# Experts' arms issued in source order: half blocks first, w2's low parts on VectorE, named PSUM banks, one tile moved behind the branch

## The chip, the cores and the metric

One core of one Trainium2 chip runs the whole program. The metric is device microseconds of an execution; lower is better. Times of before are 825.06 to 826.63 us, median 825.95 us of three runs.

## The reference

Causal attention with a bias (8 batches, 8 heads, 576 positions, 64 per head) gives 4608 tokens of 512 numbers. Each token then goes through one of eight experts, the one with the largest gate logit:

```python
for e in range(E):                       # E = 8, D = 512, F = 1024
    mask = e_idx == e
    h = np.maximum(x[mask] @ w1[e], 0.0)
    ye = h @ w2[e]
    out[mask] = gate_w[mask, None] * eom[mask, e, None] * ye
```

All of it is float32.

## The kernel before

The attention and the routing come first, in an order written by a planner (`Order`); they end at about 380 us and the change doesn't touch them. The experts then run one after the other.

**Number format.** To multiply in float32 on TensorE (PE) each operand is split into a high part and a low part of a shorter format, and three products are added: high by high, high by low, low by high. ScalarE (ACT) makes the high part with a cast, another engine the low part with a subtraction. `xh`, `xl` are the tokens (transposed), `hh`, `hl` the hidden values, `w1h`, `w1l` and `w2h`, `w2l` the weights (some tiles of both weights carry the bare name `w` in the profile). `w1r` and `w2r` are the weights as loaded, with one buffer each.

**One expert** has a front (`front`, line 1173) and a back (`back`, 1222). How many tokens an expert has is known only on the chip, so the front stands in a `Switch` with nine arms, for 512 to 768 tokens in steps of 32 (`ARMS`). Tile t is tokens 128t to 128t + 127.

- `gemm1` (847), first product: for each of NF = 8 row blocks f, 4 x 3 = 12 matmuls per half. More than 512 columns are cut into two halves u, each in its own PSUM bank of the tile `ph` (two buffers of two banks).
- `relu` (860) empties `ph`: part "h" on ACT writes `hh`, part "l" on VectorE (DVE) writes `hl`.
- `split_w2(f)` (1116) makes this expert's w2 parts from `w2r`: the cast on ACT, the subtraction on GpSimd (POOL). `split_w1(f)` (807) makes the next expert's w1 parts: the cast on ACT, the subtraction on DVE. It overwrites the parts that row block f of this expert has just used.
- `gather` (820, POOL) fetches tile f of the next expert's tokens by an indirect DMA.
- `gemm2` (1130), second product of a tile: 24 matmuls of 512 columns into a PSUM bank `py` (two buffers, taken in turn), then DVE scales it into `y` (1141), then POOL scatters `y` by an indirect DMA (1121). `gemm2_few` (1152) does a last tile of 32 or 64 tokens with the roles turned round; POOL first adds `hh` and `hl` into `hf` (1160).
- `load_w2(e + 1)` and `load_w1(e + 2)` are issued by SyncE (SP) once their buffers' readers are done.

**Front and back.** If there are more than 640 tokens (T > LT = 5) the front first transposes tile 5 (`ready`: PE transposes into `pt`, ACT makes `xh`, DVE `xl`). Then come the eight row blocks and the second product of tile 0 and of the tiles from 4 on (for expert 0, whose tiles 0 to 2 are prepared within the attention's plan, of tile 3 and those from 4 on). The back, behind the branch, does the second product of tiles 1, 2 and 3 (expert 0: tile 2), and between the matmuls of the last two it transposes the next expert's tiles 0 to 4.

**The order of the work.** The back is issued in source order (`manual_schedule`, 1239). The front is not: within an arm the framework's scheduler chooses each engine's order by its own cost model. Every engine runs its own queue in that order. Each engine takes the branches for itself, into an arm and out of it.

In this execution the experts have 544, 512, 512, 672, 704, 512, 576 and 640 tokens of room; experts 0, 3, 4 and 6 have a narrow tile.

Of the kernel before, what the change touches and what calls it, by code (L numbers as in the profile page):

```python
# [10 lines left out]
F32 = mybir.dt.float32  # L11
# [7 lines left out]
P = 128  # L19
# [192 lines left out]
def moe_attention(ctx, tc, q, k, v, s, wg, wog, w1, w2, out):  # L212
# [577 lines left out]
    def w2_lo(f, eng):  # L790
        eng.tensor_sub(w2f("l", f), w2r[:, f], w2f("h", f).bitcast(F32))  # L791
# [15 lines left out]
    def split_w1(f):  # L807
        w1_hi(f)
        w1_lo(f, nc.vector)
# [34 lines left out]
        xcopy_h(t, p)  # L844
        xcopy_l(t, p)

    def gemm1(f, c0, c1, p):

        nh = 1 if c1 - c0 <= 512 else 2
        W = (c1 - c0) // nh  # L850
        for u in range(nh):
            us = slice(c0 + u * W, c0 + (u + 1) * W)
            n = 0
            for c in range(ND):
                for a, b_ in (("h", "xh"), ("h", "xl"), ("l", "xh")):
                    nc.tensor.matmul(p[:, u, 0:W], w1f(a, f)[:, c, :], wt[b_][:, c, us],  # L856
                                     start=(n == 0), stop=(n == 3 * ND - 1))
                    n += 1

    def relu(f, c0, c1, p, part):  # L860
        nh = 1 if c1 - c0 <= 512 else 2
        W = (c1 - c0) // nh
        pv = p[:, 0:nh, 0:W]
        hv, lv = (wt[nm][:, f, c0:c1].rearrange("p (u w) -> p u w", u=nh) for nm in ("hh", "hl"))
        if part == "h":
            nc.scalar.activation(hv, pv, AF.Relu)  # L866
        else:
            nc.vector.scalar_tensor_tensor(lv, pv, 0.0, hv.bitcast(F32), ALU.max, ALU.subtract)  # L868
# [68 lines left out]
    def hint(e):  # L937
        tc.switch_hint({g: regs[e] for g in ENGINES}, (1 if e else 2) * NA, f"expert{e}")
# [176 lines left out]

    def split_w2(f):
        w2_hi(f)
        w2_lo(f, nc.gpsimd)

    def place(dst, ix, y):  # L1120
        ins = nc.gpsimd.indirect_dma_start(  # L1121
# [5 lines left out]
    def scatter(y, tb, t, m):  # L1127
        place(out, tb.bitcast(I32)[0:m, t, 1:2], y[0:m])

    def gemm2(e, t, C, between=((),)):  # L1130

        m = min(P, C - t * P)
        p = pm.tile([P, DM], F32, tag="py", name="py")
        n = NF // len(between)
        for k, steps in enumerate(between):
            for step in steps:
                step()
            product2(t, m, p, range(k * n, (k + 1) * n))
        y = mw.tile([P, DM], F32, tag="y", name="y", bufs=3)
        tb = tbs[e % 2]  # L1140
        nc.vector.tensor_scalar_mul(y[0:m], p[0:m], tb[0:m, t, 2:3])  # L1141
        scatter(y, tb, t, m)
# [6 lines left out]
        nc.sync.dma_start(tb, tab[r0:r0 + m, :].unsqueeze(0).broadcast_to([G, m, 3]))  # L1149
        return tb  # L1150

    def gemm2_few(t, m, tb):

        G = P // m
        W = DM // G
        ix = mw.tile([P, 1], I32, tag="ixf", name="ixf", bufs=2)
        nc.vector.tensor_scalar(ix, tb.bitcast(I32)[:, 1:2], float(G), grp[m], ALU.mult, ALU.add)
        hf = wt["hf"][:, :, 0:m]
        sl = slice(t * P, t * P + m)
        nc.gpsimd.tensor_add(hf, wt["hh"][:, :, sl].bitcast(F32), wt["hl"][:, :, sl].bitcast(F32))  # L1160
        p = pm.tile([P, DM], F32, tag="py", name="py")
        for f in range(NF):
            for g in range(G):
                nc.tensor.matmul(p[g * m:(g + 1) * m, 0:W], hf[:, f], w2r[:, f, g * W:(g + 1) * W],  # L1164
                                 start=(f == 0), stop=(f == NF - 1))
        y = mw.tile([P, DM], F32, tag="y", name="y", bufs=3)
        nc.vector.tensor_scalar_mul(y[:, 0:W], p[:, 0:W], tb[:, 2:3])
        place(out.rearrange("n (g w) -> (n g) w", g=G), ix, y[:, 0:W])

    def ready(t, xg):  # L1170
        xcopy(t, xtrans(xg, pm.tile([P, ND, P], F32, tag="pt", name="pt")))

    def front(e, C, early=False):


        nxt = e + 1 < E
        T = (C + P - 1) // P
        few = C % P if C % P in grp else 0
        if e == 0 and not early:
            for t in range(ET):  # L1180
                ready(t, gather(tbs[0], t, xgs[t]))
        if T > LT:
            ready(LT, wt["last"])
        c0 = min(ET * P, C - 256) if early else 0
        if few:
            places = few_places(e, T - 1, few)
        if nxt and e > 0:
            load_tab(e + 1)
        if early:
            for t in range(EY):  # L1190
                scatter(banks["ye", t], tbs[0], t, P)
        for f in range(NF):
            p = pm.tile([P, 2, 512], F32, tag="ph", name="ph")
            gemm1(f, c0, C, p)
            for part in "hl":
                relu(f, c0, C, p, part)
            if e > 0:
                split_w2(f)
            if nxt:
                split_w1(f)  # L1200
                if f < TMAX:
                    gather(tbs[(e + 1) % 2], f, xgs[f])
        if not few and nxt:
            run_all(load_w2(e + 1))
        if nxt and e + 2 < E:
            run_all(load_w1(e + 2))

        tiles = ([0] if e else [ET] if early else [ET] + list(range(EY))) + list(range(NC, T))
        if few:
            tiles.remove(T - 1)  # L1210
            tiles.insert(1, T - 1)
        for k, t in enumerate(tiles):
            if few and t == T - 1:
                gemm2_few(t, few, places)
                if nxt:
                    run_all(load_w2(e + 1))
            else:
                gemm2(e, t, C)

    xgs = {}  # L1220

    def back(e):

        if e == 0:
            where = {EY: ((0, 1), (2,), (3,), (4, "hint"))}
        else:
            where = {1: ((),), 2: ((0,), (1,)), 3: ((2,), (3,), (4,), ("hint",))}
        for t, parts in where.items():
            gemm2(e, t, CMAX, [[(lambda u=u: hint(e + 1) if u == "hint" else ready(u, xgs[u])) for u in part
                                if e + 1 < E] for part in parts])  # L1230

    rest = nc.values_load(rgi[0:1, 2 * E:2 * E + 1], min_val=0, max_val=E * NOV,
# [1 line left out]
    for e in range(E):  # L1234
        if e + 1 < E:
            xgs.update((t, xg_tile(t)) for t in range(TMAX))
        for n in tc.Switch(regs[e], (1 if e else 2) * NA, hint=f"expert{e}"):
            front(e, ARMS[n % NA], early=e == 0 and n < NA)
        with tc.manual_schedule():
            if e + 1 < E:  # L1240
                regs[e + 1] = arm_of(e + 1)
            back(e)


    with tc.If(rest > 0):
        for e in range(E):
            rv = nc.values_load(rgi[0:1, E + e:E + e + 1], min_val=0, max_val=NOV,
                                skip_runtime_bounds_check_because="counted by comparisons")
            run_all(load_w1(e))
            run_all(load_w2(e))  # L1250
            with tc.For_i(0, rv, 1) as it:
                tb = mw.tile([P, 1, 3], F32, tag="tbo", name="tbo")
                nc.sync.dma_start(tb, tab[bass.ds(it * P + (e * N + CMAX), P), :].unsqueeze(1))
                xg = sh.tile([P, DM], F32, tag=XGS[0], name="xg", bufs=1)
                nc.gpsimd.indirect_dma_start(
                    out=xg, out_offset=None, in_=xd,
                    in_offset=bass.IndirectOffsetOnAxis(ap=tb.bitcast(I32)[:, 0, 0:1], axis=0),
                    bounds_check=N, oob_is_err=False)
                p = pm.tile([P, ND, P], F32, tag="pt", name="pt")
                for c in range(ND):  # L1260
                    nc.tensor.transpose(p[:, c, :], xg[:, c * P:(c + 1) * P], ident)
                xt = sh.tile([P, ND, P], F32, tag=XGS[1], name="xto", bufs=1)
                nc.vector.tensor_copy(xt, p)
                ho = sh.tile([P, NF, P], F32, tag="kq", name="ho")
                for f in range(NF):
                    p = pm.tile([P, 2, 512], F32, tag="ph", name="ph")
                    for c in range(ND):
                        nc.tensor.matmul(p[:, 0, 0:P], w1r[:, c, f * P:(f + 1) * P], xt[:, c, :],
                                         start=(c == 0), stop=(c == ND - 1))
                    nc.vector.tensor_scalar_max(ho[:, f, :], p[:, 0, 0:P], 0.0)  # L1270
                p = pm.tile([P, DM], F32, tag="py", name="py")
                for f in range(NF):
                    nc.tensor.matmul(p, ho[:, f, :], w2r[:, f], start=(f == 0), stop=(f == NF - 1))
                y = mw.tile([P, DM], F32, tag="y", name="y", bufs=3)
                nc.vector.tensor_scalar_mul(y, p, tb[:, 0, 2:3])
                scatter(y, tb, 0, P)
# [26 lines left out]
```

## Time and profile before

| | us |
|---|---|
| median of 3 runs | 825.95 |
| profiled execution | 824.76 |
| its span, first to last instruction | 823.0 |
| PE busy | 772.9 |
| DVE busy | 473.3 |
| POOL busy | 467.1 |
| ACT busy | 441.9 |
| mean granted clock of PE, share of 2.4 GHz | 0.978 |

A record's line in order of time gives its start, its length, engine, line, operation, what it writes and reads, and, in brackets, how long the engine stood idle just before it and what ended that. Matmuls are pipelined: records overlap, so a loss of PE is read from start to start. "issue" is idle time for which the profile shows no cause; it shows above all behind the branches. Times are from the start of the span.

### The profile page before, as it was taken

To read this page: it belongs to the slowest core of one execution; us is meant where nothing else is said; L and a number is where in the kernel's file an instruction comes from. 1 tells how busy PE (TensorE), PEld (TensorE's weight loads), DVE (VectorE), ACT (ScalarE), POOL (GpSimd) and SP (SyncE) were. 2 spreads that over 40 slices of the span, in tenths; PEclk is the share of its full clock that TensorE was granted. 3 is DMA by queue.
4 is the path that set the end of the run, shared out by engine and by line. 5 is a ranking of instruction groups with operands and counts; after the bars stand their busy time and mean duration, and the time that the engine had idled before them with its cause. 6 is when DMAs were issued, how large, how long until landed. Compare 5 with 4: busy or idle time off the path is not lost.

```text
span 823.0 us, 19429 instructions
## 1 busy us (share of the span) xinstructions
PE 772.9 (94%) x6854; PEld 610.8 (74%) x6854; DVE 473.3 (58%) x1310; ACT 441.9 (54%) x1277; POOL 467.1 (57%) x691
## 2 busy tenths in 40 slices
PE   4799999999999999898979999999899999989996
PEld 2577767676777676597867877897797887978985
DVE  4688888889988889772436353251352263442211
ACT  2699999999999999741333241430431341512300
POOL 7688798988888788464226172542262171631401
PEclk9699999999999999998999999999999999999998
DMA  4878688988897884333534427216126137214001
GB/s 124 197 194 202 159 217 209 231 171 201 189 224 181 187 176 117 82 118 93 175 131 133 179 79 247 58 48 237 54 66 215 61 78 252 68 40 142 14 29 42
DMA packets 168898, 115.61 MB, mean 140 GB/s; under 512 B 128090, under 2 KB 146524, under 8 KB 168670
## 3 DMA queue, kind: packets, MB, share of 16 engines
q1 hardware_dynamic: 160590, 91.06, 42.3%
q0 software_dynamic: 8080, 22.08, 8.7%
q8 instruction: 73, 1.20, 0.6%
q14 instruction: 155, 1.27, 0.5%
HBM read 93.59 MB, written 19.65 MB: 138 GB/s over the span
## 4 chain that ended last, share of the span: by engine, by line
PE 72%; issue 12%; DVE 5%; POOL 4%; DMA 3%; ACT 1%; SPq 1%; another core or an unknown queue 1%; POOLq 0%; DVEq 0%; ACTq 0%
PE ph L856 17%; PE py L892 16%; PE O L574 9%; PE S L482 9%; PE PT L543 6%; PE S L485 4%; PE M L597 4%; PE A L404 2%; PE pt L833 2%; PE O L570 1%; POOL w L791 1%; POOL out_dram L1121 1%; PE py L1164 1%; DMA raw<-in_q_dram 1%; POOL w2l L791 1%
## 5 line engine op out<-in xcount | busy, mean ns | idle before, releaser
L1121 POOL DMA_INDIRECT out_dram<-y,tb x34 | 33.6, 989 | 195.0 <-DVE y L1141 165.9
L892 PE MATMUL py<-w,hh 128*128 128x512 f32 x420 | 133.7, 399 | 5.7 <-DVE y L1141 5.1
L482 PE MATMUL S<-kq 64*128 64x256 f32 (+3 forms) x512 | 107.7, 473 | 3.0 <-DVE m L496 2.1
L856 PE MATMUL ph<-xh,w1h 128*128 128x512 f32 (+6 forms) x312 | 105.5, 338 | 5.1 <-DVE hl L868 4.3
L856 PE MATMUL ph<-xl,w1h 128*128 128x512 f32 (+6 forms) x312 | 104.4, 335 | 3.5 <-DVE xl L841 3.4
L856 PE MATMUL ph<-xh,w1l 128*128 128x512 f32 (+6 forms) x312 | 104.2, 334 | 0.0
L837 ACT CAST xh<-pt 128x512 fp32r<-128x512 f32 x37 | 21.6, 587 | 150.7 <-PE pt L833 145.3
L892 PEld LDWEIGHTS py<-w,hh 128*128 128x128 f32 x420 | 76.6, 189 | 23.4 <-DVE y L1141 7.6
L414 ACT COPY pt<-PT 128x256 f32<-128x256 f32 (+4 forms) x261 | 90.4, 415 | 4.0 <-PE PT L543 2.5
L1141 DVE TENSOR_SCALAR y<-py,tb 128x512 f32<-128x512 f32 x33 | 24.8, 751 | 106.7 <-PE py L892 100.8
L543 PEld LDWEIGHTS PT<-ident,e 64*128 64x128 f32 x1600 | 72.2, 143 | 17.8 <-issue 8.4
L805 DVE TENSOR_TENSOR w1l<-w1r,w1h 128x512 fp32r<-128x512 f32 x46 | 54.0, 1177 | 50.4 <-ACT w1h L802 50.3
L574 PE MATMUL O<-pt,vraw 128*64 128x448 f32 (+2 forms) x512 | 82.9, 467 | 0.0
L892 PE MATMUL py<-w,hl 128*128 128x512 f32 x210 | 82.7, 394 | 0.0
L543 PE MATMUL PT<-ident,e 64*128 64x64 f32 x1600 | 77.9, 228 | 1.6 <-DVE m L496 0.9
L791 POOL TENSOR_TENSOR w<-w2r,w 128x512 fp32r<-128x512 f32 x47 | 61.1, 1312 | 19.1 <-ACT w L788 8.9
L868 DVE SCALAR_TENSOR_TENSOR hl<-ph,hh 128x512 fp32r<-128x512 f32 (+6 forms) x72 | 50.3, 701 | 35.1 <-ACT hh L866 30.2
L518 ACT ACTIVATE e<-pbB,m 128x384 f32<-128x384 f32 (+1 forms) x128 | 67.4, 529 | 3.5 <-DVE m L496 3.5
L856 PEld LDWEIGHTS ph<-xh,w1h 128*128 128x128 f32 x312 | 60.3, 193 | 11.2 <-issue 6.1
L856 PEld LDWEIGHTS ph<-xl,w1h 128*128 128x128 f32 x312 | 60.4, 193 | 7.0 <-DVE xl L841 4.3
L574 PEld LDWEIGHTS O<-pt,vraw 128*64 128x64 f32 x512 | 36.2, 139 | 38.9 <-issue 31.0
L802 ACT CAST w1h<-w1r 128x512 fp32r<-128x512 f32 x48 | 29.4, 619 | 65.6 <-issue 56.0
(180 smaller groups left out, 1831.3 us busy)
## 6 DMA issues: line engine op xcount, KB each, us to landing
cb<-cumd SPq DMA_DIRECT2D x31, 576.0 KB, 5.8
w1r<-in_moe_w_dram SPq DMA_DIRECT2D x7, 2048.0 KB
w2r<-in_moe_w_dram SPq DMA_DIRECT2D x7, 2048.0 KB, 9.8
raw<-in_k_dram SPq DMA_DIRECT2D x64, 128.0 KB, 4.3
raw<-in_q_dram SPq DMA_DIRECT2D x64, 128.0 KB, 4.1
vraw<-in_v_dram SPq DMA_DIRECT2D x64, 128.0 KB, 6.2
xd<-x SPq DMA_DIRECT2D x32, 256.0 KB, 4.9
w1r<-in_moe_w_dram SPq DMA_DIRECT2D x4, 512.0 KB, 7.2
```

Of the source, the lines that this page charges most:

```text
L414: nc.scalar.copy(out, in_)
L482: nc.tensor.matmul(d["s", t, j][:, 0:width(t)], qt[js, t * P:(t + 1) * P], kt[js, TL:TL + width(t)], start=True, stop=True)
L485: nc.tensor.matmul(d["s", t, a][js, 0:HS], d["ql"][js], kt[js, a * HS:(a + 1) * HS], start=True, stop=True)
L518: nc.scalar.activation(e[:, o:o + W], pbias(i, t, j), AF.Exp, bias=st[i].pop(("m", t, j)), scale=-1.0, accum_out=sums[i % 3][:, j, t:t + 1])
L543: nc.tensor.transpose(p[h][:, (n0 + n) * D:(n0 + n + 1) * D], d[etile(t, j)][hs, o:o + P], ident[hs, hs])
L574: nc.tensor.matmul(d["o", 1][j * D:(j + 1) * D, q0 - P:S - P], vt[:, j, c, :] if c < NM else vls[i // NPAIR % 2][:, i % NPAIR, j], pt[:, c ...
L791: eng.tensor_sub(w2f("l", f), w2r[:, f], w2f("h", f).bitcast(F32))
L805: eng.tensor_sub(w1f("l", f), w1r[:, :, f * P:(f + 1) * P], w1f("h", f).bitcast(F32))
L856: nc.tensor.matmul(p[:, u, 0:W], w1f(a, f)[:, c, :], wt[b_][:, c, us], start=(n == 0), stop=(n == 3 * ND - 1))
L868: nc.vector.scalar_tensor_tensor(lv, pv, 0.0, hv.bitcast(F32), ALU.max, ALU.subtract)
L892: nc.tensor.matmul(p[0:m], wt[a][:, f, sl], w2f(b_, f), start=(f == 0 and n == 0), stop=(f == NF - 1 and n == 2))
L1121: ins = nc.gpsimd.indirect_dma_start(out=dst, out_offset=bass.IndirectOffsetOnAxis(ap=ix, axis=0), in_=y, in_offset=None, bounds_check=dst ...
```

## The change

Within the experts only.

1. The arms are put under `manual_schedule`: issued in source order, like the back.
2. The order in an arm is written anew: `split_w2(f)` ahead of `gemm1(f)`, relu directly behind it, then `split_w1(f)` and the gather. With more than 640 tokens and two halves, the first halves of row blocks 0 and 1 go first, then their second halves; `gemm1` and `relu` take a list of halves for that.
3. The low part of w2 is made by DVE, not by POOL.
4. `py` becomes two tiles of one buffer each, `py0` and `py1`, chosen by number so that an arm's last tile has bank 0 and the first tile behind the branch bank 1.
5. Tile 3 of expert 0 moves from the arm (for the usual arms) to the back, ahead of tile 2.
6. POOL's sum for the narrow tile is cut into two, behind row blocks 5 and 7.

```diff
-        for u in range(nh):
+        for u in range(nh) if halves is None else halves:
...
     def split_w2(f):
         w2_hi(f)
-        w2_lo(f, nc.gpsimd)
+        w2_lo(f, nc.vector)
+
+    def ybank(n):
+        return pm.tile([P, DM], F32, tag=f"py{n % 2}", name="py", bufs=1)
...
+    def few_rows(t, m, f0, f1):
+        sl = slice(t * P, t * P + m)
+        nc.gpsimd.tensor_add(wt["hf"][:, f0:f1, 0:m], wt["hh"][:, f0:f1, sl].bitcast(F32), wt["hl"][:, f0:f1, sl].bitcast(F32))
...
-        nc.gpsimd.tensor_add(hf, wt["hh"][:, :, sl].bitcast(F32), wt["hl"][:, :, sl].bitcast(F32))
-        p = pm.tile([P, DM], F32, tag="py", name="py")
+        p = ybank(bank)
...
-        for f in range(NF):
+
+        def split(f):
+            if nxt:
+                split_w1(f)
+                if f < TMAX:
+                    gather(tbs[(e + 1) % 2], f, xgs[f])
+            if few and f in (5, NF - 1):
+                few_rows(T - 1, few, *((0, 6) if f == 5 else (6, NF)))
+
+        first = []
+        if T > LT and C - c0 > 512:
+
+            first = [0, 1]
+            p = [pm.tile([P, 2, 512], F32, tag="ph", name="ph") for f in first]
+            for u in range(2):
+                for f in first:
+                    if u and e > 0:
+                        split_w2(f)
+                    gemm1(f, c0, C, p[f], (u,))
+                    for part in "hl":
+                        relu(f, c0, C, p[f], part, (u,))
+                    if u:
+                        split(f)
+        for f in range(len(first), NF):
+            if e > 0:
+                split_w2(f)
             p = pm.tile([P, 2, 512], F32, tag="ph", name="ph")
             gemm1(f, c0, C, p)
             for part in "hl":
                 relu(f, c0, C, p, part)
-            if e > 0:
-                split_w2(f)
-            if nxt:
-                split_w1(f)
-                if f < TMAX:
-                    gather(tbs[(e + 1) % 2], f, xgs[f])
+            split(f)
...
-        tiles = ([0] if e else [ET] if early else [ET] + list(range(EY))) + list(range(NC, T))
+        tiles = ([0] if e else [] if early else list(range(EY))) + list(range(NC, T))
...
         for k, t in enumerate(tiles):
+            bank = len(tiles) - 1 - k
...
-            where = {EY: ((0, 1), (2,), (3,), (4, "hint"))}
+            where = {ET: ((),), EY: ((0, 1), (2,), (3,), (4, "hint"))}
...
-            front(e, ARMS[n % NA], early=e == 0 and n < NA)
+            with tc.manual_schedule():
+                front(e, ARMS[n % NA], early=e == 0 and n < NA)
```

## Rows read from the trace of the kernel before

**Rows 1.** The page, busy time: us, share of the span, instructions.
```profile
PE 772.9 (94%) x6854; PEld 610.8 (74%) x6854; DVE 473.3 (58%) x1310; ACT 441.9 (54%) x1277; POOL 467.1 (57%) x691
```

**Rows 2.** Groups by line from 386 us on, then the waits (us, times, longest).
```profile
L892 PE MATMUL py<-w,hh 128*128 128x512 f32 x396 | 126.3, 400 | 5.7 <-DVE y L1141 5.1 <-DVE y L1167 0.6
...
PE ph L856 <- DVE hl L868: 4.3, 3, 1.8
```

**Rows 3.** In order of time: PE and DVE at the end of expert 1's arm.
```profile
452.12 0.39 PE L892 MATMUL py<-w,hl 128*128 128x512 f32 x1
452.55 0.75 DVE L1141 TENSOR_SCALAR y<-py,tb 128x512 f32<-128x512 f32 x1 [3.39 <-PE py L892]
453.36 0.73 PE L892 MATMUL py<-w,hh 128*128 128x512 f32 x2 [0.85 <-DVE y L1141]
```

**Rows 4.** PE and DVE behind expert 0's branch; last, that stretch's window row (PEclk).
```profile
408.04 0.35 DVE L1167 TENSOR_SCALAR y<-py,tbf 128x128 f32<-128x128 f32 x1 [1.16 <-PE py L1164]
410.15 0.40 PE L892 MATMUL py<-w,hl 128*128 128x512 f32 x1
413.82 1.29 DVE L841 TENSOR_TENSOR xl<-pt,xh 128x512 fp32r<-128x512 f32 x2 [5.43 <-issue]
414.57 0.66 PE L833 MATMUL pt<-ident,xg 128*128 128x128 f32 x4 [4.01 <-DVE xl L841]
...
406.00:421.70 15.70, 11.56 (x110) 9.46 (x110) 4.36 (x7) 2.83 (x5) 2.04 (x2) 0.89 0.74 269
```

**Rows 5.** In order of time: PE, DVE and POOL in expert 1's first product.
```profile
421.67 0.39 PE L856 MATMUL ph<-xh,w1h 128*128 128x512 f32 x1
426.89 0.39 PE L856 MATMUL ph<-xh,w1l 128*128 128x512 f32 x1
429.11 0.47 PE L856 MATMUL ph<-xh,w1h 128*128 128x512 f32 x1 [1.83 <-DVE hl L868]
429.65 2.50 DVE L805 TENSOR_TENSOR w1l<-w1r,w1h 128x512 fp32r<-128x512 f32 x1 [0.69 <-ACT w1h L802]
430.29 1.30 POOL L791 TENSOR_TENSOR w<-w2r,w 128x512 fp32r<-128x512 f32 x1
432.90 0.47 PE L856 MATMUL ph<-xh,w1h 128*128 128x512 f32 x1 [0.78 <-DVE hl L868]
```

**Rows 6.** The same at the heads of experts 3 and 4, with one window row.
```profile
523.60 0.68 DVE L841 TENSOR_TENSOR xl<-pt,xh 128x512 fp32r<-128x512 f32 x1
524.34 0.54 PE L856 MATMUL ph<-xl,w1h 128*128 128x336 f32 x1 [1.89 <-DVE xl L841]
...
524.40:528.00 3.60, 3.60 (x14) 3.60 (x15) 0.00 (x0) 1.08 (x3) 1.82 (x3) 0.53 0.12 3
...
591.67 0.43 PE L856 MATMUL ph<-xl,w1h 128*128 128x352 f32 x1 [1.47 <-DVE xl L841]
```

**Rows 7.** The same in expert 6's first product: DVE, then PE.
```profile
722.44 3.40 DVE L805 TENSOR_TENSOR w<-w1r,w 128x512 fp32r<-128x512 f32 x1 [1.83 <-ACT w L802]
726.65 0.37 PE L856 MATMUL ph<-xh,w1h 128*128 128x288 f32 x1 [1.64 <-DVE hl L868]
```

**Rows 8.** Durations: groups by line (mean ns), two records, a DMA issue (us to landing).
```profile
L805 DVE TENSOR_TENSOR w1l<-w1r,w1h 128x512 fp32r<-128x512 f32 x42 | 49.6, 1184 | 50.4 <-ACT w1h L802 50.3
L868 DVE SCALAR_TENSOR_TENSOR hl<-ph,hh 128x512 fp32r<-128x512 f32 x24 | 16.3, 678 | 0.0
L802 ACT CAST w1h<-w1r 128x512 fp32r<-128x512 f32 x42 | 26.0, 619 | 65.6 <-issue 56.0 <-PE ph L856 6.4 <-ACT w2h L788 1.7
L866 ACT ACTIVATE hh<-ph 128x512 fp32r<-128x512 f32 x24 | 14.2, 592 | 0.0
...
390.14 0.69 DVE L805 TENSOR_TENSOR w1l<-w1r,w1h 128x512 fp32r<-128x512 f32 x1
389.41 1.00 POOL L823 DMA_INDIRECT xg<-xd,tb  x1 [0.30 <-DMA xg<-xd,tb]
...
w2r<-in_moe_w_dram SPq DMA_DIRECT2D x7, 2048.0 KB, 9.8
```

More of the change, by code (lines that the diff above doesn't have):

```diff
@@ L845, in xcopy, with gemm1 @@
         xcopy_l(t, p)
-    def gemm1(f, c0, c1, p):
+    def gemm1(f, c0, c1, p, halves=None):
         nh = 1 if c1 - c0 <= 512 else 2
         W = (c1 - c0) // nh
-        for u in range(nh):
+        for u in range(nh) if halves is None else halves:
             us = slice(c0 + u * W, c0 + (u + 1) * W)
@@ L858, in gemm1, with relu @@
                     n += 1
-    def relu(f, c0, c1, p, part):
+    def relu(f, c0, c1, p, part, halves=None):
         nh = 1 if c1 - c0 <= 512 else 2
         W = (c1 - c0) // nh
-        pv = p[:, 0:nh, 0:W]
-        hv, lv = (wt[nm][:, f, c0:c1].rearrange("p (u w) -> p u w", u=nh) for nm in ("hh", "hl"))
+        us = slice(0, nh) if halves is None else slice(halves[0], halves[-1] + 1)
+        pv = p[:, us, 0:W]
+        hv, lv = (wt[nm][:, f, c0:c1].rearrange("p (u w) -> p u w", u=nh)[:, us] for nm in ("hh", "hl"))
         if part == "h":
@@ L1128, in scatter, with gemm2 @@
         place(out, tb.bitcast(I32)[0:m, t, 1:2], y[0:m])
-    def gemm2(e, t, C, between=((),)):
+    def gemm2(e, t, C, bank, between=((),)):
         m = min(P, C - t * P)
-        p = pm.tile([P, DM], F32, tag="py", name="py")
+        p = ybank(bank)
         n = NF // len(between)
@@ L1150, in few_places, with gemm2_few @@
         return tb
-    def gemm2_few(t, m, tb):
+    def few_rows(t, m, f0, f1):
+        sl = slice(t * P, t * P + m)
+        nc.gpsimd.tensor_add(wt["hf"][:, f0:f1, 0:m], wt["hh"][:, f0:f1, sl].bitcast(F32), wt["hl"][:, f0:f1, sl].bitcast(F32))
+    def gemm2_few(t, m, tb, bank):
         G = P // m
@@ L1158, in gemm2_few @@
         hf = wt["hf"][:, :, 0:m]
-        sl = slice(t * P, t * P + m)
-        nc.gpsimd.tensor_add(hf, wt["hh"][:, :, sl].bitcast(F32), wt["hl"][:, :, sl].bitcast(F32))
-        p = pm.tile([P, DM], F32, tag="py", name="py")
+        p = ybank(bank)
         for f in range(NF):
@@ L1212, in front @@
         for k, t in enumerate(tiles):
+            bank = len(tiles) - 1 - k
             if few and t == T - 1:
-                gemm2_few(t, few, places)
+                gemm2_few(t, few, places, bank)
                 if nxt:
@@ L1217, in front @@
             else:
-                gemm2(e, t, C)
+                gemm2(e, t, C, bank)
     xgs = {}
@@ L1224, in back @@
         if e == 0:
-            where = {EY: ((0, 1), (2,), (3,), (4, "hint"))}
+            where = {ET: ((),), EY: ((0, 1), (2,), (3,), (4, "hint"))}
         else:
             where = {1: ((),), 2: ((0,), (1,)), 3: ((2,), (3,), (4,), ("hint",))}
-        for t, parts in where.items():
-            gemm2(e, t, CMAX, [[(lambda u=u: hint(e + 1) if u == "hint" else ready(u, xgs[u])) for u in part
+        for k, (t, parts) in enumerate(where.items()):
+            gemm2(e, t, CMAX, k + 1, [[(lambda u=u: hint(e + 1) if u == "hint" else ready(u, xgs[u])) for u in part
                                 if e + 1 < E] for part in parts])
@@ L1270, in moe_attention @@
                     nc.vector.tensor_scalar_max(ho[:, f, :], p[:, 0, 0:P], 0.0)
-                p = pm.tile([P, DM], F32, tag="py", name="py")
+                p = ybank(0)
                 for f in range(NF):
```

## The prediction

> **What bounds the kernel now.** I read the page first, then the groups by line, the waits, and the records in order of time around each wait. TensorE (PE) is busy for 94% of the 823.0 us span [rows 1], so only two things can give time: stretches in which PE stands still, and stretches at the lower clock. The change touches nothing ahead of the experts' arms (from about 386 us), so I looked for PE's idle time behind that point. There its matmuls of 512 columns come at a steady 0.2275 us (23 of them from 421.67 to 426.89 us [rows 5]), the twelve of a row block in 2.73 us. The groups by line and the waits name who ended the idle time: DVE's scaling of `y` 5.7 us in seven waits, and DVE's `hl` 4.3 us in three [rows 2]. In order of time the losses lie in five places, and each is priced from start to start, less the 0.23 us that a matmul takes anyway.
>
> (a) *The same PSUM bank twice.* Behind an arm's last tile, the first tile behind the branch waits until DVE has emptied the bank: the matmul at 452.12 us should be followed at 452.35 us and is followed at 453.36 us, when the 0.75 us scaling is over [rows 3]. That is 1.01 us. Six waits are like it; the seventh, behind the narrow tile of expert 6, is 0.6 us [rows 2].
>
> (b) *Expert 0 behind its branch.* PE has transposed two tiles and waits 4.01 us for `xl`, which DVE starts at 413.82 us after 5.43 us in which the profile shows nothing it waited for ("issue"): it has just taken the branch. After the wait the granted clock falls: its mean over 406 to 421.7 us is 0.89, so 15.7 x 0.11 = 1.7 us of work is lost at 1.2 GHz [rows 4].
>
> (c) *Expert 1's first product.* PE waits for `hl` twice, 429.11 - 426.89 - 0.23 = 1.99 us, and about 0.95 us at 432.90. DVE's subtraction of w1's low part, queued ahead of the next `hl`, takes 2.50 us, beside a 1.30 us subtraction on POOL [rows 5].
>
> (d) *Experts 3 and 4*, whose second halves reach into tile 5: PE does twelve matmuls of the first half and one of the second, then waits 1.89 and 1.47 us for `xl` of tile 5, again because DVE comes late out of a branch. In expert 3 the clock then falls to a mean of 0.53 over 3.6 us, 1.7 us of work [rows 6].
>
> (e) *Expert 6*: 1.64 us for `hl`, behind a w1 subtraction of 3.40 us [rows 7].
>
> **The change, part by part.**
>
> *Named banks.* The arm's last tile gets bank 0 and the first behind the branch bank 1, last used two tiles or an expert ago. Six times 1.01 plus 0.6 gives **6.7 us**. Inside an arm the banks alternate as before; a narrow tile in between takes 2 us or more of PE, longer than the 0.75 us scaling.
>
> *Tile 3 behind the branch.* Its 24 matmuls (24 x 0.2275 = 5.5 us) are only moved: in the arm they lay between row blocks at full pace and hid nothing. Behind the branch they cover DVE's 5.4 us. Counting from the end of the narrow tile: PE ends tile 3 at +5.5, DVE is back at +5.4 to +5.7, scales y until +6.5, copies the first `xl` until about +7.6; PE wants the third transpose at about +7.8. That is close, but it fits. Gain 4.0 + 0.2 + 1.7 = 5.9 us. Against it: the narrow tile now follows the last row block directly. Relu on ACT, `hl` on DVE and POOL's sum of the last two blocks need some 1.5 us, and the narrow tile's first six blocks take about that. Bounds 0 (hidden) and 1.5 (nothing hidden); I take 0.3, near hidden. So **5.6 us**.
>
> *w2's low parts from POOL to DVE.* 56 subtractions leave POOL, where one takes 1.30 us [rows 5], and join DVE's queue. On DVE the like-shaped w1 subtraction takes 0.69 us when POOL does no tensor work, on average 1.18, and up to 3.40 beside POOL's [rows 7, 8]. With POOL's gone I take 0.69 for both. Per 512-column block DVE then has 0.69 + 0.68 + 0.69 = 2.06 us, ACT 0.62 + 0.59 + 0.62 = 1.83 us (w2's cast is like w1's) [rows 8], PE 2.73: both have room, and wider blocks have more. This takes away (c) and (e): **2.9 + 1.7 us**. POOL keeps gathers, scatters and the narrow tile's sum, which now comes in two pieces with no one queued behind but the scatters.
>
> *Source order* in the arms puts relu ahead of w1's cast and one w2 split ahead of each block. What is queued behind a split that waits? On ACT and DVE the relu of that block. The split waits for the load of w2, whose landing took 9.8 us where it is shown [rows 8]; it is issued a whole second product (four tiles, over 22 us) ahead, so it costs nothing. In expert 0 the lead is shortest: tile 3 and tile 2 with five transposes, about 13 us, and the relu has another row block (2.7 us) of room. SP's table load stays at the head of the arm, and the next expert's two weight loads keep their places; POOL's gathers run earlier, since nothing stands between them.
>
> *First halves first* (experts 3 and 4). 24 matmuls of 336 columns, by 0.2275 x 336/512 = 0.15 us each, 3.6 us, now stand ahead of the first that needs tile 5, in place of 12 (1.8 us): 1.8 us more cover against waits of 1.9 and 1.5 us. DVE's `xl` is also no longer behind the narrow tile's index. Expert 3 keeps at most 0.2 us, expert 4 nothing, and without the wait the clock doesn't fall. Bounds for the clock: 0 to 1.7 us; I take it whole. 2.0 + 1.7 - 0.2 and 1.6: **5.1 us**. The second halves lead to f = 2 with a bank that is free about 0.7 us ahead.
>
> Sum: 6.7 + 5.6 + 4.6 + 5.1 = 22.0 us. The profiled execution took 824.76 us, span 823.0; the median of the runs shown is 825.95, 1.2 us more. 825.95 - 22.0 = **804.0 us**. What stays: the wait ahead of expert 0, the short waits of PE's own branches (0.3 to 0.7 us), the tail.
>
> **A rule against it.** DVE's subtractions beside a gather on POOL lasted 0.69 us, as if alone: the one at 390.14 us beside the gather from 389.41 to 390.41 us [rows 8]. The Trainium skill (SBUF — State Buffer, Who interferes with whom) states that a DVE instruction with two SBUF inputs and a GpSimd instruction that reads SBUF exclude each other for a whole instruction. For POOL's subtractions the rows agree. Read so widely that a gather, which reads its row numbers from SBUF, counts too, it speaks against moving work to DVE: rival 3; the row says no.
>
> **The rivals.**
> 1. *The banks don't matter*: the wait belongs to the joining of the arms, not to the bank, and only changes its name. Against it: the wait ends with the scaling [rows 3], and tiles 2 and 3, on alternating banks, follow without one. 804.0 + 6.7 = 810.7.
> 2. *The late returns stay ahead*: DVE comes out of the branch as late relative to the work that needs it, in experts 0 and 3, since all that comes ahead of it gets shorter too. For: margins of 0.2 us. 804.0 + 5.6 + 3.5 = 813.1.
> 3. *Gathers hold DVE*: six of about 1 us per arm. A 512-column block would want 2.06 + 1.0 us against 2.73, 0.33 us x 6 x 3 experts = 6 us: 810.0.
> 4. *Slower: DVE becomes the bound.* If a subtraction keeps lasting what it did beside POOL (2.5 us), a 512-column block wants 0.68 + 5.0 = 5.7 us of DVE against 2.73 of PE; three experts of eight blocks lose 24 x 2.95 = 71 us: 875. It decides from the point where 24 x (0.68 + 2d - 2.73) = 22 us, d = 1.48 us. Against it: POOL's subtractions are gone, and without them each shown lasted 0.69.
>
> **How the numbers follow.** Forecast 0.77, mostly 800.5 to 808.5: below 804 if the 0.3 and 0.2 us aren't paid and w1's and w2's work leaves less jitter, above it by the narrow tile (1.2 us more), expert 3's clock (1.7) and one new wait of some 1.5 us. Rival 1 0.07, rival 2 0.06, rival 3 0.03, rival 4 0.04, and 0.03 for something that eats the gain. The range 800.5 to 811.5 takes in rivals 1 and 3 and leaves out 2, 4 and the tails, about 0.18. A measurement of this kernel can tell about 0.2% from no change. Faster 0.94, same 0.02, slower 0.04.
>
> **What would show it.** Right: no matmul of the second product idle on DVE's `y`; tile 3 of expert 0 behind the branch and the transposes behind it without a 4 us hole; w1's and w2's low parts both near 0.69 us on DVE; no idle on `hl`; the granted clock at 2.4 GHz from 392 us to the tail. Wrong: DVE's subtractions over 1.4 us; ACT or DVE standing at a w2 split for a load while PE waits for `hl`; PE idle at the narrow tile of expert 0.

## The result and the profile after

The changed kernel takes 804.64 us, the median of four runs (801.46 to 805.28), beside 825.50 us for the kernel before on the same chip: a ratio of 0.974, interval 0.971 to 0.978, or 20.9 us less. The forecast was 804.0. As the experiments show, the total is right in part by luck: two terms were too large, and one that had been put at nothing was not.

The profiled execution, the fastest of the four, took 801.46 us, span 799.7, mean granted clock 0.986 (0.978 before). The page of after, busy time (us, share, instructions), for [rows 1]:

```profile
PE 763.3 (95%) x6854; PEld 607.9 (76%) x6854; DVE 478.6 (60%) x1370; ACT 442.3 (55%) x1281; POOL 393.6 (49%) x639
```

POOL lost 73.5 us of work, and DVE gained only 5.3: 56 subtractions of w2 (41 us) joined it, and those of w1 went from 68 to 38 us. The group of the second product and all waits of PE from 384 us on (us, times, longest), for [rows 2]:

```profile
L893 PE MATMUL py<-w,hh 128*128 128x512 f32 x396 | 125.5, 398 | 2.0 <-issue 2.0
...
PE py L893 <- issue: 2.0, 1, 2.0
PE pt L833 <- DMA out_dram<-y,tb: 1.1, 1, 1.1
PE ph L856 <- DVE xl L841: 1.1, 1, 1.1
PE pt L833 <- PE py L893: 0.8, 2, 0.5
PE ph L856 <- issue: 0.6, 1, 0.6
PE py L1170 <- POOL hf L1158: 0.5, 1, 0.5
PE ph L856 <- DVE hl L869: 0.3, 1, 0.3
```

No wait on DVE's `y` is left, and 0.3 us on `hl`, where there were 5.7 and 4.3. At the end of expert 1's arm, for [rows 3], PE runs past DVE's scaling (L1145) at its steady 0.23 us:

```profile
442.66 0.39 PE L893 MATMUL py<-w,hl 128*128 128x512 f32 x1
442.88 0.62 PE L893 MATMUL py<-w,hh 128*128 128x512 f32 x2
443.08 0.75 DVE L1145 TENSOR_SCALAR y<-py,tb 128x512 f32<-128x512 f32 x1 [3.47 <-PE py L893]
443.34 0.39 PE L893 MATMUL py<-w,hl 128*128 128x512 f32 x1
```

Expert 0 behind its branch, for [rows 4]; the last line is a row of the windows, whose two numbers ahead of the rate are the granted clock and the DMA share:

```profile
398.18 0.64 PE L1170 MATMUL py<-w2r,hf 128*32 128x128 f32 x16 [0.48 <-POOL hf L1158]
400.78 0.70 PE L893 MATMUL py<-w,hh 128*128 128x512 f32 x2 [1.96 <-issue]
402.23 1.05 PE L893 MATMUL py<-w,hh 128*128 128x512 f32 x2
407.95 1.04 PE L833 MATMUL pt<-ident,xg 128*128 128x128 f32 x8
...
398.00:404.00 6.00, 3.86 (x27) 2.99 (x28) 0.42 (x2) 0.00 (x0) 1.16 (x2) 0.85 0.78 275
```

The 4 us hole at the transposes is gone: eight of them run at 407.95 us without a wait. But PE now stands still ahead of tile 3, for 0.5 us at POOL's `hf` and 2.0 us behind its own branch, and from 402.2 us the pairs of matmuls take 1.05 in place of 0.62 us, at 1.2 GHz.

Expert 1's first product, for [rows 5, 8]: the window row, and 42 each of DVE's 56 subtractions for w2 (L791) and for w1 (L805), with the shortest, the median and the longest in ns:

```profile
416.00:438.00 22.00, 22.00 (x99) 18.22 (x98) 14.62 (x23) 11.97 (x23) 7.47 (x7) 1.00 0.32 86
...
L791 DVE TENSOR_TENSOR w<-w2r,w x42: 677/684/1504, 416.9 to 763.4; 128x512 fp32r<-128x512 f32 x42
L805 DVE TENSOR_TENSOR w1l<-w1r,w1h x42: 679/682/752, 387.3 to 710.6; 128x512 fp32r<-128x512 f32 x42
```

PE is busy for 22.00 of 22.00 us. Three of w2's subtractions lasted 1.09 to 1.50 us, each beside the one tensor operation that POOL kept, the narrow tile's sum. In expert 6:

```profile
704.44 1.31 POOL L1158 TENSOR_TENSOR hf<-hh,hl 128x384 f32<-128x384 f32 x1 [6.85 <-DVE hl L869]
704.80 1.50 DVE L791 TENSOR_TENSOR w<-w2r,w 128x512 fp32r<-128x512 f32 x1
```

The 44 subtractions that ran beside a gather or a scatter of POOL's took at most 0.752 us. Expert 3's head and expert 6's head, for [rows 6, 7]:

```profile
511.41 0.69 DVE L841 TENSOR_TENSOR xl<-pt,xh 128x512 fp32r<-128x512 f32 x1 [3.04 <-ACT hh L867]
512.02 0.50 DVE L869 SCALAR_TENSOR_TENSOR hl<-ph,hh 128x336 fp32r<-128x336 f32 x1
512.57 0.42 PE L856 MATMUL ph<-xh,w1h 128*128 128x336 f32 x1 [0.33 <-DVE hl L869]
...
683.45 0.37 PE L856 MATMUL ph<-xh,w1h 128*128 128x288 f32 x1 [0.56 <-issue]
```

The 1.89 us for tile 5 is down to 0.33, now on the `hl` of the first half, which stands behind tile 5's `xl` in DVE's queue, and the clock doesn't fall. Expert 6 has no more wait for `hl`, but a new 0.56 us at PE's own branch into the arm.

Start to start, the stages of the two profiled executions compare so (us):

| Stage | before | after | gain | forecast |
|---|---|---|---|---|
| seven bank waits | 6.9 | 0 | 6.9 | 6.7 |
| expert 0, first matmul of its arm to expert 1's first | 35.6 | 31.9 | 3.7 | 5.6 |
| expert 1, first product | 25.2 | 21.8 | 3.5 | 2.9 |
| experts 3 and 4, head and first product | 67.2 | 61.8 | 5.4 | 5.1 |
| expert 6, first product | 27.3 | 25.5 | 1.8, less the new 0.6 | 1.7 |
| ahead of the arms | | | 2.3 | 0 |

Of expert 0's 3.7 us, 2.6 are a stretch at 1.2 GHz at the head of its arm, which the change doesn't touch, and so are the 2.3 us ahead of the arms. One pair of executions can't carry these small terms; the runs below, five rounds each beside the kernel before on the same chip, do.

### The profile page after: what moved, and what is told of

Its sections match the earlier page's. It is cut to its first block, busy times and chain, and to the rows that moved or that the text cites. A ratio compares the mean times of both kernels' runs of the same rounds, so it can differ in the third digit from the quotient of the medians.

```text
span 799.7 us, 19332 instructions
## 1 busy us (share of the span) xinstructions
PE 763.3 (95%) x6854; PEld 607.9 (76%) x6854; DVE 478.6 (60%) x1370; ACT 442.3 (55%) x1281; POOL 393.6 (49%) x639
## 3 DMA queue, kind: packets, MB, share of 16 engines
q14 instruction: 152, 1.25, 0.5%
## 5 line engine op out<-in xcount | busy, mean ns | idle before, releaser
L867 ACT ACTIVATE hh<-ph 128x512 fp32r<-128x512 f32 (+8 forms) x76 | 44.8, 590 | 113.2 <-PE ph L856 62.9
L856 PE MATMUL ph<-xh,w1h 128*128 128x512 f32 (+6 forms) x312 | 103.2, 331 | 2.1 <-DVE xl L841 1.1
L856 PE MATMUL ph<-xl,w1h 128*128 128x512 f32 (+6 forms) x312 | 102.4, 328 | 0.1
L856 PE MATMUL ph<-xh,w1l 128*128 128x512 f32 (+6 forms) x312 | 102.4, 328 | 0.0
L869 DVE SCALAR_TENSOR_TENSOR hl<-ph,hh 128x512 fp32r<-128x512 f32 (+8 forms) x76 | 51.4, 679 | 75.7 <-ACT hh L867 75.7
L1145 DVE TENSOR_SCALAR y<-py,tb 128x512 f32<-128x512 f32 x33 | 24.8, 750 | 111.2 <-PE py L893 89.3
L856 PEld LDWEIGHTS ph<-xh,w1h 128*128 128x128 f32 x312 | 58.6, 188 | 6.3 <-issue 2.2
L823 POOL DMA_INDIRECT xg<-xd,tb x37 | 39.7, 1073 | 47.9 <-PE ph L856 22.8
L856 PEld LDWEIGHTS ph<-xl,w1h 128*128 128x128 f32 x312 | 58.7, 188 | 3.2 <-DVE xl L841 0.3
L856 PEld LDWEIGHTS ph<-xh,w1l 128*128 128x128 f32 x312 | 58.6, 188 | 2.8
```

Of the source, the lines that this page charges most:

```text
L823: ins = nc.gpsimd.indirect_dma_start(out=xg, out_offset=None, in_=xd[0:rows], in_offset=bass.IndirectOffsetOnAxis(ap=tb.bitcast(I32)[:, t, ...
```

## The experiments

Ratios are to the kernel before on the same chip (its medians were 824.7, 817.5 and 823.9 us in the three sets), so 0.01 is some 8.2 us. The change itself has 0.974 in both sets in which it ran, and a kernel of another set is compared with it by the ratios. Intervals are 5 to 8 us wide: a difference of 3 to 4 us from the change isn't clear of noise by the times alone, and there the profiles have to help.

**The banks, undone and alone.**

```diff
-        return pm.tile([P, DM], F32, tag=f"py{n % 2}", name="py", bufs=1)
+        return pm.tile([P, DM], F32, tag="py", name="py")
```

> The changed kernel with the two banks of py taken in turn again, as before the change; all else as changed. Theory (the bank is what is waited for): the seven waits of the second product on DVE's scaling come back, 1.01 us each and 0.6 behind the narrow tile of expert 6, so +6.7 us, about 811.3 us against 804.6. Rival 1 of the prediction (the wait belongs to the joining of the arms): no difference, 804.6 within 0.5, with a wait of about 1 us at the same places in both.

Measured: 0.986 (0.982 to 0.989), 9.6 us slower than the change. Six waits on `y` of 5.1 us together and one of 0.6 are back. The rest is in expert 0, which was worse in this profile, as told below. So the named banks were also put into the kernel before, with nothing else changed:

> The kernel before with the named banks of py alone. Prediction's term: -6.7 us, a ratio of 0.992. The undone change cost 1.17% of before (9.5 us, 0.9857 against 0.974), more than the term; if the banks are worth that much in the kernel before too, the ratio is 0.9885.

Measured: 0.992 (0.989 to 0.995), 6.5 us. The waits on `y` are gone from its profile. The term of 6.7 us stands, and rival 1 falls.

**Tile 3 of expert 0 back in the arm.**

```diff
-        tiles = ([0] if e else [] if early else list(range(EY))) + list(range(NC, T))
+        tiles = ([0] if e else [ET] if early else [ET] + list(range(EY))) + list(range(NC, T))
...
-            where = {ET: ((),), EY: ((0, 1), (2,), (3,), (4, "hint"))}
+            where = {EY: ((0, 1), (2,), (3,), (4, "hint"))}
```

> The changed kernel with tile 3 of expert 0 back in the arm, ahead of the narrow tile. By the prediction's term: +5.6 us, about 810.2 us, with a 4 us hole at the transposes behind the branch and the lower clock after it. By what the two traces show for expert 0 (35.6 us before, less 2.6 us that the clock took at its head, against 31.9 us after): the 0.7 us wait at the narrow tile, the 2.2 us at PE's own branch and the 1.7 us of lower clock behind it vanish as the hole comes back, so only +1 us, about 805.7 us.

Measured: 0.978 (0.974 to 0.983), 3.6 us slower than the change, between the two expectations and too wide to choose by itself. In its profile the hole at the transposes is back (DVE comes out of the branch 4.08 us late), with the lower clock behind it, and PE's waits at `hf` and behind its branch are gone:

```profile
414.88 1.29 DVE L841 TENSOR_TENSOR xl<-pt,xh 128x512 fp32r<-128x512 f32 x2 [4.08 <-issue]
415.63 0.69 PE L833 MATMUL pt<-ident,xg 128*128 128x128 f32 x2 [3.34 <-DVE xl L841]
```

The fourteen profiles give a second measure, expert 0 from the first matmul of its arm to expert 1's first: with tile 3 in the arm 35.6, 38.9, 38.1 and 39.5 us, mean 38.0 (the profile of before was the shortest of them); with tile 3 behind the branch 30.3 to 38.0 in ten profiles, mean 33.8. That is 4.3 us, but this stretch also holds a stall of ACT that comes and goes (told below) and, in some profiles, a lower clock within the first product. Less PE's idle time within the first product, and less half of the time at 1.2 GHz up to its last matmul, it is 32.8, 33.4, 33.8 and 33.0 us against 29.2 to 32.3, mean 31.0: about 2 us for the edit, an estimate.

What took the rest back is alike in all ten. From the wide matmul ahead of the narrow tile to the first matmul behind the branch PE needs 4.3 to 4.9 us, and 2.4 with tile 3 in the arm (5.3 in the kernel with source order alone, 2.9 of them at `hf`). The difference is 0.5 to 0.8 us at `hf` (in nine of the ten) and PE's own branch, which lasts 1.4 to 2.5 us in place of 0.33. The traces hold the loading of code, in 16 KB packets of an instruction queue, q8. PE's branch in the change (ns, start) and, in the window 397.4 to 397.6 us, the start of such a packet; then the same with tile 3 in the arm, window 404.4 to 404.5 us:

```profile
L1327 PEldq COMPARE_BRANCH  x1: 1893/1893/1893, 398.2 to 398.2; - x1
q8 instruction: 1, 0.02, 39.2%
...
L1327 PEldq COMPARE_BRANCH  x1: 326/326/326, 408.9 to 408.9; - x1
q8 instruction: 1, 0.02, 57.9%
```

In the change the packet lands at 398.7 us, 0.5 us into the branch, which ends 1.4 us later; with tile 3 in the arm it had landed 3.5 us ahead of the branch. The other profiles agree: of PE's 224 branches behind 390 us in the fourteen, the 106 that last over 0.5 us all end 1.25 to 1.64 us (median 1.41) behind the landing of such a packet, and ahead of a shorter one none had landed less than 1.0 us before. So the branch waits for its code.

**Both halves of a row block in a row.**

```diff
-        if T > LT and C - c0 > 512:
+        if False:
```

> The changed kernel with both halves of each row block in a row again in experts 3 and 4; all else as changed. By the prediction's term: PE waits about 2 us in each for the xl of tile 5, and the clock falls in expert 3 (1.7 us): +5.1 us, about 809.7 us. Rival: with source order DVE's xl of tile 5 comes early enough anyway, and the halves matter by under 1 us: about 805 us.

Measured: 0.978 (0.974 to 0.983), 3.6 us. The waits for tile 5's `xl` are back in experts 3 and 4, though shorter than before, and the granted clock stayed at 1.00 behind expert 3's (window row), where before it fell to a mean of 0.53:

```profile
514.44 0.69 DVE L841 TENSOR_TENSOR xl<-pt,xh 128x512 fp32r<-128x512 f32 x1 [2.94 <-issue]
515.18 0.42 PE L856 MATMUL ph<-xl,w1h 128*128 128x336 f32 x1 [1.35 <-DVE xl L841]
...
579.82 0.43 PE L856 MATMUL ph<-xl,w1h 128*128 128x352 f32 x1 [1.50 <-DVE xl L841]
...
515.20:518.80 3.60, 3.60 (x23) 3.60 (x24) 1.24 (x2) 1.48 (x3) 0.86 (x1) 1.00 0.13 7
```

So 2.9 us of wait are back in this profile, and not the 1.7 us of clock. The length of the wait doesn't decide that by itself: the clock fell behind 1.89 us in the kernel before, and stayed at 1.00 behind 2.05 us at the same place in the kernel with the banks alone. The first products of experts 3 and 4 take 63.5 us here, and 61.0 to 61.4 in the eight profiles of source order with first halves first. That makes 2.3 us; the 3.6 us of the runs aren't separated from it.

**w2's low parts and the order of the arms: four kernels in a square.** One puts w2's subtraction back on POOL, one gives the arms back to the framework's scheduler, one does both.

```diff
-        w2_lo(f, nc.vector)
+        w2_lo(f, nc.gpsimd)
```

```diff
-            with tc.manual_schedule():
+            if True:
                 front(e, ARMS[n % NA], early=e == 0 and n < NA)
```

> The changed kernel with the low part of w2 on POOL again, source order and all else as changed. Theory (DVE and POOL hold each other up when both subtract): DVE's subtractions of w1 again go up to 2.5 to 3.4 us and PE waits for hl in experts 1 and 6 at least: +4.6 us or more, about 809 us. Rival (the order did it: hl now stands right behind its matmuls and ahead of w1's split): subtractions are as long, but PE doesn't wait for them: under +1 us, about 805 us.

> The changed kernel with the arms put in order by the framework's scheduler again, as before the change; every other edit stays. The prediction gave source order nothing of its own: at most +1 us, about 805.5 us. Rival (banks, w2 on POOL, halves and tile 3, undone one at a time, cost about 8.1, 1.4, 2 and 2 us, together some 13 of the 20.9 us gained, so the rest is the order): +5 to +7 us, about 811 us, with PE's waits for hl back in the first products.

> The changed kernel with both the scheduler's order in the arms and w2's low parts on POOL: the kernel before with named banks, tile 3 moved and half blocks first. By the prediction's terms for these three, 17.4 us: a ratio of 0.979. If the scheduler's order by itself cost the 18 us that the run with it lost, the ratio stays near 0.996; then the subtractions on DVE were not the reason.

Measured ratios, with banks, tile 3, halves and the cut sum of the change in all four:

| Order of the arms | w2 on POOL | w2 on DVE |
|---|---|---|
| the scheduler's | 0.983 (0.978 to 0.988) | 0.997 (0.994 to 0.999) |
| source order | 0.978 (0.974 to 0.981) | 0.974, the change |

Read across, DVE's work on w2 *costs* 11 us under the scheduler and brings 2.9 us in source order, which isn't clear of noise. Read down, source order brings 18.5 us with DVE, and 4.5 us with POOL, where the intervals overlap. Together they bring 7.3 us, where the prediction had 4.6, all of it put down to the engine and none to the order. The profile of the scheduler's order with DVE says why. In expert 1 (DVE, then PE, then the wait in all from 378 us on):

```profile
418.27 2.55 DVE L791 TENSOR_TENSOR w<-w2r,w 128x512 fp32r<-128x512 f32 x4 [0.26 <-ACT w L788]
420.74 1.28 DVE L791 TENSOR_TENSOR w2l<-w2r,w2h 128x512 fp32r<-128x512 f32 x2
421.94 0.68 DVE L805 TENSOR_TENSOR w1l<-w1r,w1h 128x512 fp32r<-128x512 f32 x1
422.54 0.68 DVE L869 SCALAR_TENSOR_TENSOR hl<-ph,hh 128x512 fp32r<-128x512 f32 x1
...
423.37 0.47 PE L856 MATMUL ph<-xh,w1h 128*128 128x512 f32 x1 [0.71 <-DVE hl L869]
...
PE ph L856 <- DVE hl L869: 13.1, 9, 2.8
```

The subtractions are as short as in the change (4 in 2.55 us), but the scheduler lines up six of w2 and one of w1 ahead of the first `hl`. PE waits 13.1 us in nine places, and in experts 3, 4 and 7 the clock falls to 1.2 GHz behind such a wait (2.84, 2.84 and 2.33 us; in expert 6 it doesn't, behind 2.33 us). It isn't DVE's time that was short but the place of `hl` in DVE's queue. With POOL and source order, on the other hand, the subtractions of w1 beside POOL's again last up to 2.48 us (mean 0.88, against 0.68 in the change and 1.22 before), and PE waits for `hl` twice in the arms, 3.2 us of it in expert 0 at the stall told below and 0.6 in expert 3. So the rival's account fits this profile: long subtractions hardly hold PE up when `hl` stands ahead of them.

**Source order alone, in the kernel before** (the same two lines of `manual_schedule`, nothing else).

> The kernel before with its arms issued in source order and nothing else: w2's low part stays on POOL, banks in turn, tile 3 in the arm, both halves in a row. If the order takes away the waits for hl by itself (hl stands right behind its matmuls, whatever the subtractions take), the 4.3 us of them go: a ratio of 0.994 to 0.995. If order and DVE's work on w2 are only worth something together (with the scheduler's order the changed kernel lost 2.2%, mostly by hl behind w2's subtractions on DVE), no difference: 0.998 to 1.002.

Measured: 1.012 (1.007 to 1.017), 9.7 us *slower*, which neither theory expected. The waits for `hl` are down to 1.5 us as the first one said, but a new one is there, in four places:

```profile
PE py L1164 <- POOL hf L1160: 14.3, 4, 5.0
...
553.31 1.03 POOL L1121 DMA_INDIRECT out_dram<-y,tb  x1 [3.76 <-DVE ixf L1157]
554.37 0.72 POOL L1160 TENSOR_TENSOR hf<-hh,hl 128x256 f32<-128x256 f32 x1
...
552.28 0.75 DVE L1141 TENSOR_SCALAR y<-py,tb 128x512 f32<-128x512 f32 x1 [2.18 <-PE py L892]
...
555.15 0.87 PE L1164 MATMUL py<-w2r,hf 128*32 128x128 f32 x12 [2.91 <-POOL hf L1160]
```

In the source of before, POOL's sum for the narrow tile stands inside `gemm2_few`, behind the scatter of the tile ahead of it. In source order POOL therefore waits for DVE, whose scaling of that tile's `y` ends at 553.03 us (the row names the index `ixf`, which DVE makes directly behind it), issues the scatter, and only then makes `hf`, for which PE has been waiting. The scheduler had moved the sum forward. In the change, whose sixth edit cuts the sum in two and issues it behind row blocks 5 and 7, 0.5 us of this wait is left. No run undoes that edit alone; the prediction gave it one clause and no price.

**The change once more, and the stall of ACT in expert 0.** Several profiles showed PE waiting for `hl` in expert 0's arm. In the kernel with the banks undone, ACT, then PE:

```profile
386.91 0.61 ACT L802 CAST w1h<-w1r 128x512 fp32r<-128x512 f32 x1
390.06 0.38 ACT L867 ACTIVATE hh<-ph 128x256 fp32r<-128x256 f32 x1 [2.54 <-PE ph L856]
394.38 0.39 ACT L867 ACTIVATE hh<-ph 128x256 fp32r<-128x256 f32 x1 [3.42 <-remote]
...
395.27 0.39 PE L856 MATMUL ph<-xh,w 128*128 128x256 f32 x1 [2.63 <-DVE hl L869]
```

PE had finished the block that the second relu reads at about 389.6 us; the relu starts at 394.38, and no row shows what ACT waits for ("remote" stands for another core or an unknown queue).

> The changed kernel, once more. Its first profile, of an execution of 801.5 us, shows no wait of PE for hl in expert 0's arm, while the four kernels that undo a part show 1.5 to 4.6 us of it there, behind an ACT that stands still for 2 to 4 us with nothing to wait for. If that stall belongs to those kernels, this one is free of it again, at 801 to 802 us. If it comes and goes in any kernel and the first profile was a lucky execution, this profile shows it too and the time is 804 to 806 us.

> The changed kernel with the gathers of expert 0's arm two row blocks later (behind blocks 2 to 7 in place of 0 to 5). If ACT's stall in that arm comes from the gathers that run back to back on POOL and on the DMA engines beside it, the stall is gone or comes later, and the time is 801 to 802 us. If it has another cause (code that arrives late, whatever the gathers do), the profile shows 1.5 to 4.6 us of waits for hl there as before, at 804 to 806 us.

Measured: the change again 0.974 (0.971 to 0.976), its profile with 0.9 us of such waits; with the gathers later 0.974 (0.972 to 0.977), and none. In the fourteen profiles the loss at these waits runs from 0 to 5.1 us, with tile 3 in the arm or not, and in the second set of runs all four kernels had 1.0 us or less. So it comes and goes, and the gathers can't be told from chance by these runs. Code that arrives late is unlikely: in three of the four profiles with a wait for "remote" (banks, tile 3, w2 on POOL) no packet of an instruction queue moves while ACT stands still. The cause stays open.

**An earlier hint, and `hf` from the bank.** The hint tells each engine which arm comes next. The first kernel gives it some 3.9 us earlier (PE: 4.8 us ahead of its branch into expert 3, in place of 0.9):

```diff
-            where = {1: ((),), 2: ((0,), (1,)), 3: ((2,), (3,), (4,), ("hint",))}
+            where = {1: ((),), 2: ((0,), (1,)), 3: ((2,), ("hint", 3), (4,), ())}
```

> The changed kernel with the branch hint for the next arm one transposed tile and two quarter products earlier in the backs of experts 1 to 6 (some 3.7 us more ahead of the branch). If PE's, ACT's and DVE's time to come into an arm other than the smallest (2.5 to 3.8 us each in experts 3, 4, 6 and 7) is the fetch of its code that the hint starts too late, these times shrink, PE's waits of 0.4 to 0.7 us at the entry of the four arms go, and the time falls by 2 to 3 us. If the hint doesn't matter, or what was fetched is lost again before the branch, no difference, or up to 2 us slower.

Measured: 0.973 (0.970 to 0.976), 796.3 us beside 797.5 for the change on the same chip, which isn't clear of noise. Entering expert 6, the change (first two rows) and the earlier hint (last two):

```profile
679.40 0.39 PE L893 MATMUL py<-w,hl 128*128 128x512 f32 x1
680.21 0.37 PE L856 MATMUL ph<-xh,w1h 128*128 128x288 f32 x1 [0.42 <-issue]
```

```profile
676.25 0.39 PE L893 MATMUL py<-w,hl 128*128 128x512 f32 x1
676.48 0.29 PE L856 MATMUL ph<-xh,w1h 128*128 128x288 f32 x1
```

PE's branches into experts 3, 4, 6 and 7 last 3.5, 3.5, 3.7 and 3.4 us in the change and 0.4, 1.9, 1.8 and 0.7 us here; the waits there are gone. The code packet lands 1.9 to 2.3 us behind the start of the branch in the change, and here from 1.2 us ahead of it to 0.5 us behind. ACT's and DVE's time to come in stays at 2.5 to 2.7 and 2.8 to 3.4 us. The Trainium skill (Runtime: NRT & Kernel Launch, Instruction fetch mechanics) states that a taken branch whose target isn't in the current window of code fetches it by DMA before going on. PE's rows agree; ACT's hint came 3.3 us earlier too (3.5 us ahead of its branch in place of 0.2) and gained nothing, which it doesn't explain.

The second kernel adds to that, for expert 0 alone:

```diff
+            if few and not e and f >= 6:
+                ...
+                nc.vector.tensor_scalar_max(wt["hf"][:, f, 0:few], p[:, a // W, a % W:a % W + few], 0.0)
```

> The changed kernel with the earlier hint in the backs, and in expert 0 the narrow tile's last two row blocks of hf made by DVE straight from the bank in place of POOL's sum. PE's 0.5 us wait for POOL's hf goes, the entries of experts 3, 4, 6 and 7 lose 2 to 3 us as in the run with the hint alone: a ratio of 0.971 to 0.973 against 0.974 of the change. If the hint's gain was scatter: 0.974.

Measured: 0.971 (0.966 to 0.976), the lowest ratio of all, but not separated from the change. The wait for POOL's `hf` is gone, and the one behind it, at PE's own branch, is 2.3 us in place of 2.0: the code packet lands 1.2 us into this branch, so getting there sooner gains nothing. The earlier hint didn't hold up either: with the same hint as in the kernel above, PE's branches into experts 3, 4, 6 and 7 last 0.4, 3.3, 3.6 and 0.5 us, so in two of four as long as with the late one. What decides when the code comes isn't shown.

## Why the prediction was right, and where it was not

Adding the parts in steps, each a ratio measured above:

| Step | ratio | us | forecast |
|---|---|---|---|
| banks, on the kernel before | 1 to 0.992 | 6.5 | 6.7 |
| tile 3, halves (and the cut sum) on top | to 0.983 | 7.6 | 10.7 |
| source order and w2 on DVE on top | to 0.974 | 7.3 | 4.6 |

The last two steps carry some 5 us either way, so it is the profiles that tell the terms apart.

- *Named banks*: right in mechanism and size.
- *Tile 3 behind the branch*: the hole it was to fill went, as forecast, but the term was too large. It was 5.6 us; the runs give 3.6, not clear of noise, and the profiles about 2. The step that failed is the price of what it uncovers on PE: the prediction set 0.3 us against the gain, for the narrow tile alone. The narrow tile costs 0.7 us, and behind it PE's own branch lasts 1.9 us where it lasted 0.3 (2.0 us of idle time), because its code lands only then. In six of the ten profiles with tile 3 behind the branch the clock also falls behind that wait, so that part of the 1.7 us isn't gained. The prediction had left PE's own branches as "short waits" of 0.3 to 0.7 us. Two of its own signs came out against it here: PE idle at the narrow tile of expert 0, and a stretch at 1.2 GHz behind 392 us.
- *First halves first*: right in mechanism; 2.3 us by the profiles and 3.6 by the runs, against 5.1. Part of that term came from the other edits: with both halves in a row the waits were 1.35 and 1.50 us and brought no lower clock. The 1.7 us for the clock, taken whole although the bounds were 0 to 1.7, was luck in the kernel before: of three profiles with a wait of 1.35 to 2.05 us there, one shows the fall.
- *w2's low parts on DVE*: the duration taken (0.69 us) was right, the median is 0.684 us, and w1's fell to 0.682; only the three beside POOL's remaining sum were longer. The step that failed is the one behind it. "Both have room" compared DVE's time per block with PE's, and source order was then costed as moving things at no price. The square shows that the room is worth nothing without the order: with the same short subtractions and the scheduler's order the kernel is 11 us slower than with POOL. Order and engine together gave 2.7 us more than the term, which isn't clear of noise.
- *Rival 1* falls with the banks alone. *Rival 2* came true for a small part: 0.33 us at expert 3's head, and in the second profile of the change 0.78 us at expert 0's transposes. *Rival 3* falls: the 44 subtractions beside a gather or a scatter last at most 0.752 us. The Trainium skill (SBUF — State Buffer, Who interferes with whom), read so widely that a gather counts, isn't borne out; for POOL's subtractions the rows agree, 2.48 us beside them and 0.75 without. *Rival 4* falls with the same rows, yet with the scheduler's order DVE did hold PE up and ate most of the gain, by another way: not long subtractions but short ones in the wrong place.
- The waits that came new: 1.3 us in expert 3's back, where PE and DVE both wait until 558.2 us for a DMA of the scatters, and the 0.6 us at expert 6's entry. The profile names the scatter as what ended the first. Why the transposes need it was not tried.

```profile
558.20 0.66 PE L833 MATMUL pt<-ident,xg 128*128 128x128 f32 x4 [1.14 <-DMA out_dram<-y,tb]
558.28 0.75 DVE L1145 TENSOR_SCALAR y<-py,tb 128x512 f32<-128x512 f32 x1 [5.87 <-DMA out_dram<-y,tb]
```

## What to carry to other kernels

Moving work to an engine that has time is only half an edit: look at what stands in its queue ahead of the result that the bottleneck waits for, because by that alone the same move cost 11 us or brought some 3. Before an order is fixed by hand, walk every engine's queue for steps that the scheduler had moved forward; here one small sum left behind a scatter cost 14 us of waits. And price the bottleneck's own branch, from when its code lands and from what is queued ahead of it: in the change PE's branch out of expert 3's arm lasts 2.8 us (from 547.4 us on) and costs nothing, as wide matmuls are still queued, and the one out of expert 0's arm lasts 1.9 us behind the narrow tile and costs 2.0.

## What the runs showed of the hardware

- Coming out of or into an arm is an engine's own time, and differs by engine: PE 0.3 to 3.9 us; in the change ACT 0.4 us into the smallest arm and 2.5 to 2.7 us into those of experts 3, 4, 6 and 7; DVE up to 6.5 us out of one.
- A branch of PE that lasts over 0.5 us ends some 1.4 us behind the landing of a 16 KB packet of code (106 branches of 106), and a hint given 4.8 us ahead of the branch instead of 0.9 shortened six branches of eight in two kernels.
- ACT can stand still for 3.4 to 4.1 us in expert 0's arm with nothing that the profile names, in some executions and not in others.
- A subtraction on DVE that runs beside POOL's is lengthened more or less by when each is issued: with the two splits issued together (source order in the kernel before) w1's lasted 1.41 us on average, with w2's a row block ahead (the change on POOL) 0.88.
